# Block sums of phase 2 kept in three PSUM banks, an eleventh weight slot and new planner rules in a fused attention and MLP kernel

## The chip, the cores and the metric

The kernel runs on one core of a Trainium2 chip. The metric is the device time of one execution in microseconds; the median of several runs is compared. The engines are PE (TensorE, matrix products), DVE (VectorE), ACT (ScalarE), POOL (GpSimd) and SP (SyncE, which issues the DMAs).

## The reference

Windowed causal attention with a linear bias per head, then two blocks of dense layers on its 2304 rows. All inputs are float64.

```python
# q, k, v: 4 batches, 8 heads, 576 positions, 64 channels
mask = (rel >= 0) & (rel < 128)
scores = np.where(mask, q @ k.T / 8 - slope[h] * abs(rel), -1e9)
attn = softmax(scores)
x = (attn @ v) as (2304, 512)
h = (x @ w1) * (x @ w2) @ w3          # 512 -> 1024, 1024 -> 1024
x = h @ w_out                         # 1024 -> 512
h = np.maximum(x @ w_in, 0)           # 512 -> 2048
out = h * h @ w_out2                  # 2048 -> 512
```

## The kernel before

**How the work is tiled.** Every tile has 128 partitions. A product of two matrices that must be exact to about float32 is written by `mm3` (L170) as three matmuls on parts called hi and lo (L171 to L173: hi by hi, hi by lo, lo by hi). The weights arrive as float64 words and are turned into float32 on the chip: `conv_g` on ACT (L294), `conv_s` on DVE or ACT (L296), `conv_m` on DVE (L309); a copy (L176, L224) makes hi, and a subtraction (`sub`, L179) makes lo.

**Attention** takes the 32 heads in 16 pairs, `add_pair` (L499). A pair of heads has on PE the scores qk (L428, three pieces, 64 rows of contraction), for each head nine transposes of the exponentials (`p_tr`, L444, in two parts, 4 and 5), and pv (L460, two halves, 64 output columns); on DVE the row maxima (`l_min`, L395), row sums (L410, L411) and scaling (L218), on ACT the exponentials (L403) and the copies of the transposes (`l_pt`, L176). In the same stretch PE forms the product w3 times w_out (`p_w34`, L564): 64 products of 128x128 by 128x512, each in two passes that show as two instructions. It reads the words' converted halves in place, so every other 32-bit word of a row of `raw`. PE's other filling there is batch 0 of x @ w1, x @ w2 and their product with w3·w_out.

**Phase 1** (from about 239 us) does the same for batches 1 to 3 with seven block products instead of eight (Strassen-Winograd): `add_sab` (L968) sums them in three PSUM banks al, be and ga; ACT copies a bank into the buffer d while PE goes on in another, and DVE adds the copies (L1008) and multiplies (L1014). The combined weight blocks are made by `add_wmake` (L897): `combine` (L773) adds 256-column blocks on DVE or POOL, whichever the planner takes.

**Phase 2** (from about 484 us) has two kinds of groups that `add_group` (L1053) writes. The 24 r groups (j, m) compute relu(x @ w_in) for 384 tokens a block, each with seven products P1 to P7 of six matmuls. The nine o groups compute the second layer for 256 columns, 24 matmuls a product. `add_group` gives each product a PSUM bank X of its own (six in all); ACT copies P1's bank (c1), and DVE makes the four blocks of the result by seven additions (L1083): u2 = c1 + P6, u3 = u2 + P7, u4 = u2 + P5, c22 = u4 + P7, c11 = c1 + P2, c12 = u4 + P3, c21 = u3 + P4. For r, ACT then takes the relu of each block in place (L1109), and SP stores it (`s_scr`); the o groups load it again into fo, square it (L1161 and L1147) and split it into words ww or st. In the first o group each product is cut in two (Q and P), so that its first part can run before the last words are ready.

**The order of the work.** All of it is put in order by `Plan` (L32 to L126). A task has a rank, a cost on each engine that may take it (`w_mm`, `w_tt`, `w_act`, ... , L229 to L249), the tasks it depends on, and the buffers it takes and gives back. `run` steps through time: among the tasks that could start within LOOK = 0.1 of the earliest, the one with the lowest rank is next, on the engine where it ends first. The number of buffers for each tag is a table ahead (L253). The engines then run their instructions in exactly this order. `RANK["h0"] + 20.0 * m` is the rank of the m-th pair of heads, `RANK["w34"]` that of the words for L564.

Of the kernel before, what the change touches and what calls it, by code (L numbers as in the profile page):

```python
# [15 lines left out]
RANK = dict(w34=5.49, h0=-13.66, w12=35.93, w12s=7.96, w12l=7.68, mg=500, mgs=4, yl=8, yn=0)  # L16
# [7 lines left out]
NE = 3  # L24
# [3 lines left out]
OM = 3  # L28


class Plan:
# [7 lines left out]
    LOOK = 0.1  # L39

# [15 lines left out]
    def run(self):  # L56
# [14 lines left out]
        order = []  # L71
        while ready:
            cands = []
            for n in ready:
# [29 lines left out]
            _, _, fn, deps, takes, gives, _ = tasks[n]  # L104
            ready.remove(n)
# [18 lines left out]
        assert len(order) == len(tasks), [n for n in tasks if n not in end][:20]  # L124
# [4 lines left out]
def fused_kernel(  # L129
# [119 lines left out]
    def w_dma(kb, n=1):  # L249
# [4 lines left out]
            u=10, u34=4, wo=4, qk=2, v=2, e=NE, p4=4, s=4, t=1, pt=NE, a=1, g=2, asb=2, gf=2, gt=8, ye=2,  # L254
            al=2, be=2, ga=2, d1=2, d2=2, d4=2, gq=8, xs=2, xm=1, xt1=1, xt2=1, yA=14, yB=6, s0=1, t2a=1, t2b=1, v6=6, st=2, c1=2, U2=1, U4=1, U3=1, C=4, X=6, fo=4, fq=5, ww=4,
# [16 lines left out]
    def slot(tag="u"):  # L272
        p, n = (wp, 10) if tag == "u" else (p34, 4)
        return p.tile([128, 2, 1024], F32R, tag=tag, bufs=n, name="wu")

    def w_load(key):
# [4 lines left out]
        else:  # L281
            t = wp.tile([128, 1024, 2], U32, tag="u", bufs=10, name="raw")
# [42 lines left out]
    def add_words(key, rank, tag, users, keep, lead, side=False):  # L325
# [5 lines left out]
        add("cn" + k, rank, {"D": 1.16}, lambda e: conv_m(key, flat(raws[key]) if side else None), ["cg" + k, "cs" + k])  # L331
# [157 lines left out]
    def p_warm():  # L489
        t = ps_t.tile([128, 512], F32, tag="t", name="t")  # L490
        for _ in range(4):
            nc.tensor.matmul(t[:, 0:256], ident, bm[:, 0], start=True, stop=True)
# [6 lines left out]
    def add_pair(m, rank):  # L499
# [17 lines left out]
        for g, w in enumerate((448, 512, 192)):  # L517
            add(f"qk{g}_{m}", r + 1, {"pe": w_nat(w) + 0.1}, lambda e, g=g: p_qk(m, g), [f"ldq{n}" for n in heads] + last,
# [22 lines left out]
        for g, w in enumerate((640, 384)):  # L541
            add(f"pv{g}_{m}", r + 8, {"pe": w_nat(w) + 0.1}, lambda e, g=g: p_pv(m, g),
# [15 lines left out]
    def p_w34(fi, c):  # L558
# [3 lines left out]
        wl = f(raws["w3", fi][:, c * 128:(c + 1) * 128, 0])  # L562
        wr = f(raws["wo", c // 2][:, (c % 2) * 512:(c % 2) * 512 + 512, 0])
# [139 lines left out]
    PO = (1, 6, 7, 5, 2, 3, 4)  # L703
# [7 lines left out]
    def open_q1():  # L711
# [185 lines left out]
    def add_wmake(fi, b, users, rank, prev):  # L897
# [5 lines left out]
        for i in range(4):  # L903
            add(f"cb{i}{z}", rank, w_tt(256), lambda e, i=i: combine("A", i, M, Sg, e),
                ["mb" + z] + [[], [f"cb0{z}"], [f"cb0{z}"], [f"cb1{z}"]][i], [], ["st" + z])
        for part, w in (("a", 1024), ("b", 768)):
# [132 lines left out]
    def p_r(j, m, P):
        o = p_bank(("r", j, m), P, TN)  # L1040
        wh, wl = w_of("i", m, P)
        for c in range(2):
            y = yo[j, P, c]
            mm3(o, wh[:, 128 * c:128 * c + 128], wl[:, 128 * c:128 * c + 128], y[:, 0], y[:, 1], c == 0, c == 1)

    def p_o(t, P, c0=0, c1=NM):
        o = p_bank(("o", t), P, 256) if c0 == 0 else bank[("o", t), P]
        a = ow[t, P]
        for c in range(c0, c1):
            bh, bl = w_of("o", c, P)  # L1050
            mm3(o, a[:, 0, 128 * c:128 * c + 128], a[:, 1, 128 * c:128 * c + 128], bh, bl, c == 0, c == NM - 1)

    def add_group(g, n, order, prod, fin, rank):  # L1053

        z = "".join(str(x) for x in g)
        lastq = list(lastp)
        w = 24 * w_mm(256) if g[0] == "o" else 6 * w_mm(TN)
        for nm, k in (("c1", 2), ("U2", 2), ("U3", 1), ("U4", 2)):
            hold(nm + z, nm, k)
        for c in ("11", "12", "21", "22"):  # L1060
            hold(f"C{c}{z}", "C", 1)
        for i, P in enumerate(order):
            deps, gives, fn = prod(P)
            hold(f"X{P}{z}", "X", 2 if P == 7 else 1)
            if g == ("o", 0):
                add(f"Q{P}{z}", rank + i, {"pe": 18 * w_mm(256)}, lambda e, P=P: p_o(0, P, 0, 6),
                    [d for d in deps if d[-2:] not in ("o6", "o7")] + [lastq[0]], [f"X{P}{z}"])
                lastq[0] = f"Q{P}{z}"
# [290 lines left out]
```

## Time and profile before

| | |
|---|---|
| runs | 857.64, 858.53, 858.99 us; median 858.53 us |
| profiled execution | 858.35 us; span of its trace 856.6 us, mean granted clock 0.992 |
| PE busy | 830.9 us (97%), 5808 matmuls |
| DVE, ACT, POOL busy | 676.9 (79%), 473.6 (55%), 118.4 us (14%) |
| DMA | 139 MB, mean 162 GB/s |

The span runs from the first to the last instruction. An engine's busy time says how long it had work in it; where PE's is short of a stretch, something made it wait. A granted clock of 1.00 is 2.4 GHz, one of 0.50 is 1.2 GHz.

### The profile page before, as it was taken

Reading aid. Unit: us, or ns where it says so; the run is one execution under the profiler, and the core shown is the slowest. Engines: PE = TensorE matmul, PEld = TensorE weight load, DVE = VectorE, ACT = ScalarE, POOL = GpSimd, SP = SyncE. Lnnn points to the kernel's source line nnn. Section 1 sums busy time; section 2 is a strip of 40 time slices with the busy share of each in tenths; the row PEclk is TensorE's granted clock in tenths of the full one; section 3 lists DMA queues with packets and bytes.
Section 4 is the critical chain, followed back from the end, with each engine's and each line's share of the span. In section 5 each row is a group of like instructions: output and inputs, shape, how many; then the busy total and the mean of one; then the engine's idle time right before and its main releaser. Section 6 shows DMA issues by size and latency. Waiting matters only on the chain.

```text
span 856.6 us, 15632 instructions
## 1 busy us (share of the span) xinstructions
PE 830.9 (97%) x5808; PEld 755.5 (88%) x5808; DVE 676.9 (79%) x1417; ACT 473.6 (55%) x961; POOL 118.4 (14%) x133
## 2 busy tenths in 40 slices
PE   6899999999999999999999999999999899999998
PEld 4444477877999989999998999999999799999998
DVE  6889898778599897789468798765689988977772
ACT  5856679988733344343144455543676675665440
POOL 1000000000021320040022053230257200000000
PEclk7999999999999999999999999999999999999999
DMA  9875984686542356511124165343686565545210
GB/s 299 312 240 218 286 269 125 201 242 214 209 169 88 95 173 207 191 51 39 53 79 140 49 217 176 127 164 112 205 275 205 163 162 148 156 135 144 85 49 26
DMA packets 92924, 139.17 MB, mean 162 GB/s; under 512 B 8368, under 2 KB 70320, under 8 KB 90800
## 3 DMA queue, kind: packets, MB, share of 16 engines
q1 hardware_dynamic: 92848, 138.18, 50.3%
q8 instruction: 45, 0.74, 0.4%
q14 instruction: 31, 0.25, 0.1%
HBM read 95.29 MB, written 42.86 MB: 161 GB/s over the span
## 4 chain that ended last, share of the span: by engine, by line
PE 79%; DVE 11%; DMA 4%; ACT 3%; issue 3%; POOL 0%; SPq 0%; ACTq 0%; DVEq 0%; POOLq 0%
PE X L173 14%; PE X L171 14%; PE X L172 14%; PE g L564 6%; PE g L171 5%; PE g L173 4%; PE g L172 4%; PE s L428 3%; PE t L444 3%; PE a L460 3%; DMA u<-in_w2io_dram 2%; PE al L985 2%; PE al L987 2%; PE al L986 2%; DVE d L1008 1%
## 5 line engine op out<-in xcount | busy, mean ns | idle before, releaser
L773 POOL TENSOR_TENSOR st<-st 128x256 f32<-128x256 f32 x65 | 57.3, 894 | 250.7 <-DMA st<-m_scrc 77.6
L1109 ACT ACTIVATE C<-C 128x384 f32<-128x384 f32 x96 | 48.2, 522 | 59.6 <-DVE C L1083 33.7
L171 PE MATMUL g<-gt,wu 128*128 128x288 f32 x256 | 76.3, 298 | 0.0
L172 PE MATMUL g<-gt,wu 128*128 128x288 f32 x256 | 75.6, 296 | 0.0
L173 PE MATMUL g<-gt,wu 128*128 128x288 f32 x256 | 75.4, 295 | 0.0
L403 ACT ACTIVATE e<-e,st 128x256 f32<-128x256 f32 (+1 forms) x128 | 60.6, 476 | 17.5 <-DVE st L395 16.8
L1083 DVE TENSOR_TENSOR C<-X,U 128x384 f32<-128x384 f32 (+1 forms) x99 | 50.6, 518 | 22.4 <-PE X L173 19.4
L172 PE MATMUL X<-yA,u 128*128 128x384 f32 x192 | 65.0, 339 | 0.0
L171 PE MATMUL X<-yA,u 128*128 128x384 f32 x192 | 65.0, 339 | 0.0
L564 PE MATMUL g<-raw 128*128 128x512 f32 x128 | 63.7, 626 | 1.4 <-DVE raw L309 1.4
L173 PE MATMUL X<-yA,u 128*128 128x384 f32 x192 | 65.0, 339 | 0.0
L985 PE MATMUL al<-x,wc 128*128 128x288 f32 x192 | 57.8, 301 | 3.6 <-ACT d L176 3.6
L176 ACT ACTIVATE ww<-fq 128x1024 fp32r<-128x1024 f32 x35 | 37.0, 1059 | 38.2 <-PE X L173 28.2
L986 PE MATMUL al<-x,wc 128*128 128x288 f32 x192 | 56.6, 295 | 0.3 <-DVE x L179 0.3
L987 PE MATMUL al<-x,wc 128*128 128x288 f32 x192 | 56.8, 296 | 0.0
L172 PE MATMUL X<-u,ww 128*128 128x256 f32 x198 | 55.4, 280 | 0.0
L173 PE MATMUL X<-u,ww 128*128 128x256 f32 x198 | 55.4, 280 | 0.0
L171 PE MATMUL X<-u,ww 128*128 128x256 f32 x198 | 55.4, 280 | 0.0
L395 DVE CUSTOM_DVE_ANT_0 e<-s,bm 128x256 f32<-128x256 f32 (+1 forms) x128 | 43.7, 387 | 13.3 <-PE s L428 8.0
L176 ACT ACTIVATE d<-al 128x288 f32<-128x288 f32 x72 | 29.1, 409 | 41.6 <-PE al L987 32.8
L179 DVE TENSOR_TENSOR ww<-fq,ww 128x1024 fp32r<-128x1024 f32 x35 | 42.8, 1222 | 11.0 <-ACT ww L176 10.7
L171 PEld LDWEIGHTS g<-gt,wu 128*128 128x128 f32 x256 | 48.1, 188 | 0.8 <-issue 0.8
(216 smaller groups left out, 2728.3 us busy)
## 6 DMA issues: line engine op xcount, KB each, us to landing
s_scr<-C SPq DMA_DIRECT2D x96, 192.0 KB, 2.2
u<-in_w2io_dram SPq DMA_DIRECT2D x26, 512.0 KB, 6.1
fo<-s_scr SPq DMA_DIRECT2D x20, 512.0 KB, 4.3
qk<-in_qk_dram SPq DMA_DIRECT2D x32, 288.0 KB, 5.2
st<-m_scrc SPq DMA_DIRECT2D x18, 512.0 KB, 3.7
raw<-in_w3t_dram SPq DMA_DIRECT2D x8, 1024.0 KB, 7.7
raw<-in_w_dram SPq DMA_DIRECT2D x8, 1024.0 KB, 9.0
fq<-s_scr SPq DMA_DIRECT2D x16, 512.0 KB, 4.3
```

The lines of the kernel that those rows point to most:

```text
L171: nc.tensor.matmul(o, wh, xh, start=start, stop=False)
L172: nc.tensor.matmul(o, wh, xl, start=False, stop=False)
L173: nc.tensor.matmul(o, wl, xh, start=False, stop=stop)
L176: nc.scalar.activation(out=o, in_=i, func=ACTF.Copy)
L403: nc.scalar.activation(out=e, in_=e, func=ACTF.Exp, bias=st[:, 0, i:i + 1], scale=-1.0, accum_out=st[:, 1, i:i + 1],)
L564: nc.tensor.matmul(gw[fi], wl, wr, start=c == 0, stop=c == 7)
L773: ENG[e].tensor_tensor(out=o, in0=a, in1=b, op=op)
L985: nc.tensor.matmul(o, wh, xh, start=start and c == 0, stop=False, skip_group_check=True)
L986: nc.tensor.matmul(o, wh, xl, start=False, stop=False, skip_group_check=True)
L987: nc.tensor.matmul(o, wl, xh, start=False, stop=c == 1, skip_group_check=True)
L1083: nc.vector.tensor_tensor(out=t_(o, tag), in0=bank[g, P], in1=cs[g, i], op=ALU.add)
L1109: nc.scalar.activation(out=x, in_=x, func=ACTF.Relu)
```

## The change

In phase 2, `add_group` keeps three banks instead of seven: P1 goes to bank xa, and P6, P5 and P3 are added to it by PE itself; P7 goes to xb, P4 is added; P2 goes to xc. Before PE adds the next product to xa, ACT or DVE copies what stands there (c1, u2 and u4), and the last copy is c12, for r with the relu in it. DVE then has three additions a group (c22, c11, c21). In the last r group and the first o group P4 has a bank xd in place of the second half of xb, and four additions. The products' order is now 1, 2, 6, 7, 5, 3, 4. One more weight slot is paid for by one p4 buffer and one xs buffer less; the first o group's second word takes it. `conv_m` writes the words of w3 and w_out side by side. The planner charges 0.11 for a change between the tile shapes of qk, pv and the rest and then stays with a shape, and before its time 40 it fills gaps on PE of over 1 us with small products (`filler`, 11 in all). Pairs of heads are 12 ranks apart instead of 20 and begin at -20, the words for L564 at 4. Two more o words (m = 3, 4) are not merged ahead of time. `combine` in `add_wmake` is tied to DVE: of 72 such additions 32 were on POOL.

```diff
-RANK = dict(w34=5.49, h0=-13.66, w12=35.93, w12s=7.96, w12l=7.68, mg=500, mgs=4, yl=8, yn=0)
+RANK = dict(w34=4, h0=-20, w12=35.93, w12s=7.96, w12l=7.68, mg=500, mgs=4, yl=8, yn=0, hs=12)
-OM = 3
+OM = 5
...
+    SWITCH = 0.11
+    STAY = 60
+    FILL = 40.0
...
+        shape = lambda n: {"qk": 1, "pv": 2}.get(n[:2], 0)
...
+                    if e == "pe" and shape(n) != now:
+                        w += self.SWITCH
+                    elif e == "pe" and now:
+                        rank -= self.STAY
...
+            if e == "pe":
+                now = shape(n)
+                idle = t - free.get(e, t)
+                if 1.0 < idle and t < self.FILL:
...
+                            tasks[k] = (0, {}, lambda e, tag=tag, idle=idle: self.filler(tag, int((idle - 0.4) / 0.24), 128), (), (), (), 0)
...
-            u=10, u34=4, wo=4, qk=2, v=2, e=NE, p4=4, s=4, ...
+            u=11, u34=4, wo=4, qk=2, v=2, e=NE, p4=3, s=4, ...
-            ... v6=6, st=2, c1=2, U2=1, U4=1, U3=1, C=4, X=6, ...
+            ... v6=6, st=2, xa=2, xb=2, xc=2, D1=2, D2=2, D4=2, D3=1, ...
...
-        add("cn" + k, rank, {"D": 1.16}, lambda e: conv_m(key, flat(raws[key]) if side else None), ["cg" + k, "cs" + k])
+        add("cn" + k, rank, {"D": 1.16}, lambda e: conv_m(key, flat(raws[key])), ["cg" + k, "cs" + k])
...
-        wl = f(raws["w3", fi][:, c * 128:(c + 1) * 128, 0])
-        wr = f(raws["wo", c // 2][:, (c % 2) * 512:(c % 2) * 512 + 512, 0])
+        wl = f(flat(raws["w3", fi]))[:, c * 128:(c + 1) * 128]
+        wr = f(flat(raws["wo", c // 2]))[:, (c % 2) * 512:(c % 2) * 512 + 512]
...
-            add(f"cb{i}{z}", rank, w_tt(256), ...
+            add(f"cb{i}{z}", rank, w_tt(256, "D"), ...
...
+        for nm, tag in (("xa", "xa"), ("xb", "xb"), ("xc", "xc"), ("C11", "D1"), ("C21", "D2"), ("C22", "D4"), ("C12", "D3")):
+            hold(nm + z, tag, 1)
+        steps = [
+            (1, "xa", [], True), (2, "xc", [], True), (6, "xa", ["c1"], False), (7, "xb", [], True),
+            (5, "xa", ["u2"], False), (3, "xa", ["u4"], False), (4, "xb", ["c22"], False),
+        ]
+        if last:
+            hold("xd" + z, "xc", 1)
+            p4 = (4, "xd", [], True)
+            steps = [*steps[:2], steps[3], p4, steps[2], *steps[4:6]] if g[0] == "r" else [*steps[:2], p4, *steps[2:6]]
+        for i, (P, nm, dep, first) in enumerate(steps):
             deps, gives, fn = prod(P)
...
+            deps = deps + [d + z for d in dep] + {6: [f"P1{z}"], 5: [f"P6{z}"], 3: [f"P5{z}"], 4: [f"P7{z}"]}.get(P, [])
...
+        def cp(e, c, tag, func=None):
+            t = cs[g, c] = new(tag, [128, TN])[:, 0:n]
+            if func:
+                nc.scalar.activation(out=t, in_=bank[g, "xa"], func=func)
+            else:
+                copy(e, t, bank[g, "xa"])
+
+        for nm, P, c, tag in (("c1", 1, "11", "D1"), ("u2", 6, "21", "D2"), ("u4", 5, "22", "D4")):
+            add(nm + z, -30, w_copy(n, True), lambda e, c=c, tag=tag: cp(e, c, tag), [f"P{P}{z}"], [f"C{c}{z}"])
...
+        plus("c22", "22", "xb", ["u4", "P7"], [], -30)
+        plus("c11", "11", "xc", ["c1", "P2"], ["xc"], -20)
+        if last:
+            plus("d21", "21", "xb", ["u2", "P7", "c22"], ["xb"], -20)
+            plus("c21", "21", "xd", ["d21", "P4"], ["xd"], -20)
+        else:
+            plus("c21", "21", "xb", ["u2", "P4", "c22"], ["xb"], -20)
+        if g[0] == "r":
+            add("c12" + z, -20, w_act(n), lambda e: cp(e, "12", "D3", ACTF.Relu), [f"P3{z}"], [f"C12{z}"], [f"xa{z}"])
...
-            tag = "st" if P in (1, 2) else "ww"
+            tag = "u" if (t, P) == (0, 2) else "st" if P in (1, 2) else "ww"
...
-        add_pair(m, RANK["h0"] + 20.0 * m)
+        add_pair(m, RANK["h0"] + RANK["hs"] * m)
```

The planner's order shows in the instructions. PE at the program's start, before, behind the warming product L492: L428 is a piece of qk, L444 transposes, L564 the first product of w3 and w_out.

```order
L428 MATMUL s<-qk 128x128 x2
L428 MATMUL s<-qk 128x256 x6
L428 MATMUL s<-qk 128x192 x2
L444 MATMUL t<-ident,e 128x128 x4
L444 MATMUL t<-ident,p_140 128x128 x2
L444 MATMUL t<-ident,e 128x128 x7
L428 MATMUL s<-qk 128x128 x2
L428 MATMUL s<-qk 128x256 x2
L444 MATMUL t<-ident,p_141 128x128 x2
L444 MATMUL t<-ident,e 128x128 x3
L428 MATMUL s<-qk 128x256 x4
L564 MATMUL g<-raw 128x512
```

The first product of w3 and w_out stands after one pair's scores, two heads' transposes and most of the next pair's scores.

PE at the start, with the change (L515, L451, L467, L483 and L589 are the same lines, moved):

```order
L515 MATMUL t<-bm,ident 128x256 x4
L451 MATMUL s<-qk 128x128 x2
L451 MATMUL s<-qk 128x256 x6
L515 MATMUL t<-bm,ident 128x128 x2
L451 MATMUL s<-qk 128x192 x2
L451 MATMUL s<-qk 128x128 x2
L451 MATMUL s<-qk 128x256 x6
L467 MATMUL t<-ident,e 128x128 x4
L451 MATMUL s<-qk 128x192 x2
L467 MATMUL t<-ident,p_138 128x128 x2
L467 MATMUL t<-ident,e 128x128 x3
L515 MATMUL g<-bm,ident 128x128 x3
```

The second pair's scores have moved ahead of the second head's transposes, small fillers (L515) have come in, and the first product of w3 and w_out (L589) stands only 18 rows below these, after the third pair's scores and the first pv.

DVE in the r groups, before, one group from its first addition (U and c are the intermediate sums, X the banks):

```order
L1083 TENSOR_TENSOR U_6601<-X,c_6591 128x384
L1083 TENSOR_TENSOR U_6610<-X,U_6601 128x384
L1083 TENSOR_TENSOR U_6619<-X,U_6601 128x384
L1083 TENSOR_TENSOR C<-X,U_6619 128x384
L1083 TENSOR_TENSOR C<-X,c_6591 128x384
L1083 TENSOR_TENSOR C<-X,U_6619 128x384
L1083 TENSOR_TENSOR C<-X,U_6610 128x384
```

Three of the seven make intermediate sums, and four of them read one.

DVE in the r groups, with the change, two groups (D holds the copies and becomes the result):

```order
L1122 TENSOR_TENSOR D_6303<-xb,D_6303 128x384
L1122 TENSOR_TENSOR D_6287<-xb,D_6287 128x384
L1122 TENSOR_TENSOR D_6312<-xc,D_6312 128x384
L1122 TENSOR_TENSOR D_6366<-xb,D_6366 128x384
L1122 TENSOR_TENSOR D_6350<-xb,D_6350 128x384
L1122 TENSOR_TENSOR D_6375<-xc,D_6375 128x384
```

A group has three additions where it had seven, and none of them adds onto another.

ACT in the r groups, before: c1's copy, and relus (L1109) between conversions of the stage.

```order
L176 ACTIVATE c_7179<-X 128x384
L1109 ACTIVATE C<-C 128x384
L1147 ACTIVATE fo<-fo 128x1024
L176 ACTIVATE u<-s_7013 128x1024
L176 ACTIVATE v_7234<-s_7013 128x768
L1109 ACTIVATE C<-C 128x384 x2
L176 ACTIVATE u<-st 128x1024
```

Only the copy of P1 (c) reads a bank here.

ACT in the r groups, with the change (L199 the copies of xa, L1113 the copy with the relu in it, L1152 the other relus):

```order
L199 ACTIVATE D_6350<-xa 128x384
L199 ACTIVATE D_6366<-xa 128x384
L199 ACTIVATE D_6375<-xa 128x384
L1152 ACTIVATE D_6366<-D_6366 128x384
L1113 ACTIVATE D_6384<-xa 128x384
L1152 ACTIVATE D_6350<-D_6350 128x384
L1152 ACTIVATE D_6375<-D_6375 128x384
```

Seven instructions of a group follow one another on ACT, four of which read xa between PE's products into it.

## Rows read from the trace of the kernel before

**Rows 1.** Groups of the page: busy us of each engine (share of the span) x instructions.
```profile
PE 830.9 (97%) x5808; PEld 755.5 (88%) x5808; DVE 676.9 (79%) x1417; ACT 473.6 (55%) x961; POOL 118.4 (14%) x133
```

**Rows 2.** Stretches: us; busy of PE, PEld, DVE, ACT, POOL; PEclk; DMA; GB/s.
```profile
6.40:28.00 21.60, 16.60 (x87) 10.51 (x86) 16.24 (x61) 15.50 (x45) 0.00 (x0) 0.76 0.91 305
28.00:53.00 25.00, 21.81 (x116) 11.85 (x117) 23.02 (x61) 19.49 (x45) 0.80 (x2) 1.00 0.75 284
...
115.00:239.00 124.00, 123.48 (x1015) 101.44 (x1014) 98.03 (x401) 106.64 (x319) 1.33 (x3) 1.00 0.67 205
239.00:484.00 245.00, 237.82 (x1759) 234.01 (x1758) 200.61 (x371) 93.14 (x184) 43.10 (x44) 1.00 0.34 114
484.00:667.00 183.00, 183.00 (x1052) 183.00 (x1052) 137.51 (x229) 99.18 (x182) 66.42 (x63) 1.00 0.53 177
667.00:680.00 13.00, 9.13 (x56) 8.60 (x56) 12.74 (x15) 8.27 (x12) 2.83 (x3) 0.87 0.36 108
```

**Rows 3.** PE waits: engine, tile, line, releaser: us in total, times, longest.
```profile
PE al L985 <- ACT d L176: 3.6, 5, 1.2
```

**Rows 4.** Timeline of DVE, 8 to 17 us: start, us, engine, line, operation, tiles.
```profile
8.21 0.29 DVE L395 CUSTOM_DVE_ANT_0 e<-s,bm 128x128 f32<-128x128 f32 x1 [3.13 <-PE s L428]
...
14.06 0.17 DVE L410 TENSOR_SCALAR st<-st 128x5 f32<-128x5 f32 x1
...
15.93 0.69 DVE L303 TENSOR_SCALAR raw<-raw 128x1024 uint32<-128x1024 uint32 x1
16.54 1.22 DVE L309 SCALAR_TENSOR_TENSOR raw<-raw 128x1024 uint32<-128x1024 uint32 x1
```

**Rows 5.** Groups by line and shape: count, busy us, mean ns, idle before.
```profile
L773 DVE TENSOR_TENSOR st<-st 128x256 f32<-128x256 f32 x51 | 21.8, 460 | 2.0 <-DMA st<-m_scrc 1.7
...
L176 ACT ACTIVATE c<-X 128x384 f32<-128x384 f32 x24 | 11.6, 482 | 3.0 <-PE X L173 2.9
```

**Rows 6.** Groups by line and shape, PE, 6.4 to 53 us.
```profile
L564 PE MATMUL g<-raw 128*128 128x512 f32 x28 | 15.0, 641 | 1.4 <-DVE raw L309 1.4
```

**Rows 7.** Timeline of PE, transposes and a pv half.
```profile
41.47 0.76 PE L460 MATMUL a<-pt,v 128*64 128x192 f32 x8
...
44.20 0.60 PE L444 MATMUL t<-ident,e 128*128 128x128 f32 x4
44.63 1.07 PE L564 MATMUL g<-raw 128*128 128x512 f32 x2
```

**Rows 8.** Timeline of PE, qk visits between products of w3 and w_out.
```profile
56.05 11.97 PE L564 MATMUL g<-raw 128*128 128x512 f32 x26
67.95 1.79 PE L428 MATMUL s<-qk 64*128 64x128 f32 x16
69.67 2.08 PE L564 MATMUL g<-raw 128*128 128x512 f32 x4
71.68 0.60 PE L428 MATMUL s<-qk 64*128 64x192 f32 x4
72.20 1.18 PE L564 MATMUL g<-raw 128*128 128x512 f32 x2
```

**Rows 9.** Timeline of DVE and POOL, 311 to 317 us.
```profile
311.89 0.45 DVE L224 CAST x<-xm 128x576 fp32r<-128x576 f32 x1
...
316.47 1.00 DVE L224 CAST x<-xm 128x576 fp32r<-128x576 f32 x1
...
314.99 2.17 POOL L773 TENSOR_TENSOR st<-st 128x256 f32<-128x256 f32 x2
```

**Rows 10.** Timeline of phase 1, 455 to 460 us, PE and ACT.
```profile
456.08 0.39 ACT L176 ACTIVATE d<-al 128x288 f32<-128x288 f32 x1
...
456.53 0.40 PE L985 MATMUL al<-x,wc 128*128 128x288 f32 x1 [1.04 <-ACT d L176]
...
457.30 0.30 PE L987 MATMUL al<-x,wc 128*128 128x288 f32 x1
...
457.69 0.41 ACT L176 ACTIVATE d<-al 128x288 f32<-128x288 f32 x1 [1.22 <-PE al L987]
```

More of the change, by code (lines that the diff above doesn't have):

```diff
@@ L71, in run @@
         order = []
+        shape = lambda n: {"qk": 1, "pv": 2}.get(n[:2], 0)
+        now = 0
         while ready:
@@ L123, in run @@
                     ready.add(u)
-        assert len(order) == len(tasks), [n for n in tasks if n not in end][:20]
+        assert len(order) == len(tasks) and len(end) + sum(n[:4] == "fill" for n in tasks) == len(tasks), [n for n in tasks if n not in end][:20]
         return order
@@ L323, in flat, with add_words @@
         return r.rearrange("p n w -> p (n w)")[:, 0:1024]
-    def add_words(key, rank, tag, users, keep, lead, side=False):
+    def add_words(key, rank, tag, users, keep, lead):
         k = "%s%d" % key
@@ L487, in t_xs, with p_warm @@
         nc.sync.dma_start(out=x_scr[b][p], in_=xt[b, p])
[L489 to L492, printed above, removed]
+    def p_warm(tag="t", k=4, w=256):
+        t = (ps_t if tag == "t" else ps_g).tile([128, 512], F32, tag=tag, name=tag)
+        for _ in range(k):
+            nc.tensor.matmul(t[:, 0:w], ident, bm[:, 0, 0:w], start=True, stop=True)
+    plan.filler = p_warm
     hold("warm", "t", 1)
@@ L517, in add_pair @@
         for g, w in enumerate((448, 512, 192)):
-            add(f"qk{g}_{m}", r + 1, {"pe": w_nat(w) + 0.1}, lambda e, g=g: p_qk(m, g), [f"ldq{n}" for n in heads] + last,
+            add(f"qk{g}_{m}", r + 1, {"pe": w_nat(w)}, lambda e, g=g: p_qk(m, g), [f"ldq{n}" for n in heads] + last,
                 [f"s{g}_{n}" for n in heads], [f"qk{m}"])
@@ L1050, in p_o, with add_group @@
             bh, bl = w_of("o", c, P)
[L1051 to L1053 removed]
+            mm3s(o, a[:, 0, 128 * c:128 * c + 128], a[:, 1, 128 * c:128 * c + 128], bh, bl, start and c == 0, c == NM - 1)
+    def add_group(g, n, prod, fin, rank, last=False):
         z = "".join(str(x) for x in g)
[L1056 removed]
         w = 24 * w_mm(256) if g[0] == "o" else 6 * w_mm(TN)
[L1058 to L1062, printed above, removed]
[L1063 to L1093 removed]
@@ new lines, in add_group, with go @@
+        for i, (P, nm, dep, first) in enumerate(steps):
+            deps, gives, fn = prod(P)
+            deps = deps + [d + z for d in dep] + {6: [f"P1{z}"], 5: [f"P6{z}"], 3: [f"P5{z}"], 4: [f"P7{z}"]}.get(P, [])
+            if P == 1 and lastp[0]:
+                deps = deps + lastp
+            if P == 1:
+                lastp[0] = f"P1{z}"
+            def go(e, P=P, nm=nm, first=first, fn=fn, **kw):
+                if first and not kw.get("c0"):
+                    bank[g, nm] = new("xc" if nm == "xd" else nm, [128, 512])[:, 0:n]
+                fn(bank[g, nm], first, **kw)
+            if g == ("o", 0) and P in (1, 2):
+                add(f"Q{P}{z}", rank + i, {"pe": 0.75 * w}, lambda e, go=go: go(e, c0=0, c1=6),
+                    [d for d in deps if d[-2:] not in ("o6", "o7")], [nm + z])
+                add(f"P{P}{z}", rank + i, {"pe": 0.25 * w}, lambda e, go=go: go(e, c0=6, c1=NM), deps + [f"Q{P}{z}"], [], gives)
+            else:
+                add(f"P{P}{z}", rank + i, {"pe": w}, go, deps, [nm + z] if first else [], gives)
@@ new lines, in cp, with plus @@
+        def cp(e, c, tag, func=None):
[6 more added lines that the diff above has]
+            add(nm + z, -30, w_copy(n, True), lambda e, c=c, tag=tag: cp(e, c, tag), [f"P{P}{z}"], [f"C{c}{z}"])
+        def plus(nm, c, b, deps, gives, rank):
+            def fn(e):
+                nc.vector.tensor_tensor(out=cs[g, c], in0=bank[g, b], in1=cs[g, c], op=ALU.add)
+            add(nm + z, rank, w_tt(n, "d"), fn, [d + z for d in deps], [], [b + z for b in gives])
@@ L1189, in add_o @@
             early = -30 if t == 0 and P in (1, 2) else 0
-            add(f"oh{P}{t}", rank + pos + early, w_act(1024), hi, [src[P]] + ([] if tag == "st" else ["q2"]) + (["wlao6", "wlbo6"] if t == 0 and tag == "st" else [])
+            add(f"oh{P}{t}", rank + pos + early, w_act(1024), hi, [src[P]] + ([] if tag != "ww" else ["q2"]) + (["wlao6", "wlbo6"] if t == 0 and tag != "ww" else [])
                 + chain[P], [f"ow{P}{t}"], F(k))
```

93 lines of the change are left out of this document (43 added, 50 removed).

## The prediction

> **What bounds the kernel now.** The first thing to read is the page's line of engines: PE (TensorE) is busy 830.9 us of a span of 856.6 [rows 1]. So the time can fall only where PE idles, runs at its lower clock, or spends longer on an instruction than its columns need. Next comes the table of stretches, to find where that is [rows 2]. Three stretches hold nearly all of it. From 6.4 to 28 us PE is busy 16.60 of 21.60 us at a mean granted clock of 0.76 (1.2 GHz for part of it), and to 53 us another 21.81 of 25.00. From 239 to 484 (phase 1) it idles 245 - 237.82 = 7.2 us. From 667 to 680, where phase 2 turns from the r groups to the o groups, it is busy 9.13 of 13.00 at 0.87. The r groups (484 to 667) keep PE busy all of 183.00 us. Read last, the list of PE's waits says who ends phase 1's idle times: first of all ACT's copies of its sums, 3.6 us in five waits [rows 3].
>
> The sum is made against the profiled execution, 858.35 us (span 856.6 plus 1.75 around it), 0.18 under the median of 858.53. About 0.2%, or 1.7 us, is what a measurement here can tell from no change.
>
> **The change, part by part.** PE loses no product and gains 11 small filler matmuls, so every term is idle time or overhead.
>
> *Start.* In the old order PE takes the first w3·w_out product (L564) after two pairs of heads have begun; in the new one three pairs of qk, almost four heads' transposes and one pv pair come first. What PE must wait for is DVE. Its prices: ten row maxima of two heads from 8.21 to 11.74, 1.76 per head; row sums and scaling of a head from 14.06 to 15.93, 1.87; a word conversion 0.69 and 1.22 [rows 4]. Ahead of the conversion of the fourth w_out word (cnwo3), the new DVE order has 41 maxima (14.5), scaling for 7.5 heads (14.0), six and seven of the two conversion steps (12.7) and six adds to x, taken at 0.46 like the adds of [rows 5] (2.8): 44.0 us from 8.21, so about 52 us. By then PE has all that needs neither this word nor later ones. Counted against what PE did by 53 in the old trace (28 L564 instructions, so 14 products of two each [rows 6]; likewise three qk pairs and six heads' transposes), that is nine transposes for each of two heads more, about 1.0 per head (four take 0.43), one second pv half at about 0.8 [rows 7], the first pieces of two qk pairs at 1.72 and one last piece at 0.5, and three products fewer at 2 x 0.458 [rows 8]: 2.0 + 0.8 + 3.44 + 0.5 - 2.75 = 4.0 us of work. PE is full from 53 on, so work done earlier comes off the end: **-4.0**. Bounds: 0, if ACT's exponentials (busy 35 of these 46.6 us) replace DVE as the gate, and -8.6, all 8.2 us idle of 6.4 to 53 and a little of the lower clock. The four groups of fillers stand in idle gaps ahead of the first product and count as nothing; without a gap each would cost two or three short matmuls.
>
> *Fewer changes of tile shape.* The planner now charges a change between qk's (64 rows), pv's (64 columns) and the full tile, and PE makes 114 instead of 126. A row prices one: 26 L564 take 11.90 us, 0.458 each; four between two qk visits take 71.68 - 69.67 = 2.01 where 1.83 would do, so 0.18 [rows 8]. 12 x 0.18 = **-2.2**; bounds -1 and -3.
>
> *Later attention.* With pairs 12 instead of 20 ranks apart and filled from earlier, the same exponentials, copies and maxima fall into some 205 us instead of 233; ACT then has about 84% and DVE 90%, as ACT has now from 115 to 239 (106.64 of 124, with PE idle only 0.5) [rows 2]. **+1.5**, between 0 and +6.
>
> *w3 and w_out words side by side.* L564 costs 0.458 us for 512 columns; if it went at the rate of the r groups' products (183.00 us for 1052, nearly all of 384 columns [rows 2]: 0.453 ns per column, four times that for the four passes of one product, 1.81 ns, against 1.79 now) it gains nothing; at that of the qk visits it gains 2.9 us: the visit of 16 takes 1.72 us and the one of four 0.52 [rows 8], so 1.20 us for the 704 columns between them (two heads run side by side), 1.70 ns, and 0.09 x 512 x 64 products is 2.9 us. I take **-1.0**; bounds 0 and -2.9. The Trainium skill (SBUF — State Buffer, in "Door 1: The DMA port swizzle") says that reads run at full bandwidth with two hits per 16-byte line, and so that up to four fp32 words may be strided for free; every other word would then cost nothing, and the forecast would be 1.0 higher. The rows above cannot tell 0 from 2.9.
>
> *Phase 1.* All 72 of its 256-column combinations are now on DVE, 32 more than before: 32 x 0.46 [rows 5] = 15 us on an engine with 200.61 of 245 busy [rows 2]. Against that POOL makes none of them any more: while POOL adds (from 314.99) DVE's cast takes 1.00, without it 0.45 [rows 9]. POOL's 43.1 us in this stretch slow DVE by up to as much, so the exchange should at least pay for itself, and 3.6 us of PE waiting for ACT's copies here are late DVE work handed on [rows 3]. **-2.0**; bounds -6 and +5.
>
> *r groups.* Seven banks with seven adds become three chains: P1, P6, P5, P3 in one, P7, P4 in another, P2 alone. DVE has 95 adds fewer of 168; ACT has 72 copies more and 24 relus fewer, which are folded into the last copy. DVE's relief is worth nothing here, since PE has no idle time [rows 2]. But P5 now waits for ACT's copy after P6, and P3 for the one after P5: 48 waits that did not exist. One product of another bank lies between, six matmuls of 0.174 = 1.05 us. The hand-over costs 0.09 (PE's end at 457.60 to ACT's start at 457.69) plus 0.48 (copy of 384 columns) plus 0.06 (copy's end at 456.47 to PE's start at 456.53) [rows 5, 10]: 0.63, so 0.4 us are free unless ACT is at something else. Its longer pieces, copies of 1024 columns, can be in front. Phase 1 already hands over in this way, and loses 7.2 us over 24 groups. I take **+1.5** (two or three collisions in every ten groups), bounds 0 and +9.8, a whole rate of 0.2 for each hand-over. The eleventh u slot frees its loads sooner; PE waits for none there: 0.
>
> *The turn.* o's first two products now run in part ahead of r's last, and P4 has a bank of its own; but P6 and P5 of o's first group stand behind DVE, which splits the same words. Idle of 3.9 us and 0.13 x 13 = 1.7 us for the lower clock [rows 2] become idle of about 4.8, an estimate from three conversions and splits in a row on DVE, and one on ACT: **-0.8**, between -4 and +3.
>
> *o groups, end.* One o product is 24 matmuls of 256 columns, at 0.453 ns a column 2.8 us, against a hand-over of 0.6: 0. The last add stays.
>
> Sum: -4.0 - 2.2 + 1.5 - 1.0 - 2.0 + 1.5 - 0.8 = -7.0, so 858.35 - 7.0 = 851.35, **851.4 us**; bounds of the terms, not all at one end, give 844 to 857.
>
> **The rivals.** *The chain decides (slower).* The 48 hand-overs of the r groups wait for ACT: each copy is queued behind a conversion of 1024 columns or a relu, as ACT works 99.18 of 183 us here already and gets 72 copies more for 24 relus fewer, about 48 x 0.48 = 23 us. At 0.3 us each they cost 14.4 instead of 1.5: 851.4 + 12.9 = 864.3. At 0.18 each, 8.5 over all, the whole gain is gone. For it: phase 1's waits. Against it: the planner gives these copies the first rank, and 0.4 us of each is covered. *The start gives nothing.* Heads taken first only bring ACT and DVE to their limit later, the 4.0 comes back as waits between 100 and 210, and the fillers are not enough to raise the clock: 851.4 + 4.0 and 1.5 more of the later waits = 856.9, about the same as before. For it: ACT is 86% busy from 115 to 239. Against: PE has no idle time there now, and the words are converted as early as before to within a few us. *More goes than I count.* The losses of phase 1 (7.2 us) and of the turn (5.6) go to half, and the L564 take their whole 2.9: 851.4 - (3.6 - 2.0) - (2.8 - 0.8) - 1.9 - 5.0, the last from the start's lower clock and idle time, = 840.9. That needs DVE to be freed from POOL's adds by more than the 15 us that it takes over.
>
> **How the numbers follow.** The forecast 0.50 (844 to 857, all but its last 0.2 us faster); the chain 0.17; no gain at the start 0.17, two thirds of it within 1.7 us of before; more than counted 0.16. From 841 to 862 leaves out half of the chain's case and half of the largest gain, some 0.17. Faster by over 0.2%: 0.50 + 0.16 + 0.03 = 0.69; same 0.12; slower 0.17 + 0.02 = 0.19.
>
> **What would show it.** Right: PE's busy time within 3 us of 830.9; more qk and transposes and fewer L564 before 53 us; idle in phase 1 under 5 us; r groups at 183 to 185 us; L564 at about 0.45 each. Wrong: PE waiting for ACT's copy of xa in most r groups (the chain), or PE waits on pt or e between 100 and 210 us that together pass 3 us (the start), or a stretch 239 to 484 that is longer than before. A time over 858 or under 844 makes the forecast wrong.

## The result, and the profile after

The changed kernel takes 846.04 us (median; 845.36 to 847.64) against 858.09 in the same comparison: a ratio of 0.9862 (95% interval 0.9843 to 0.9881), 12 us. The direction and the range were as forecast; the gain is 12 where 7.0 were expected. The profiled execution took 845.38 us, with a span of 843.4.

The page's line of engines, to be read beside [rows 1]:

```profile
PE 823.2 (98%) x5830; PEld 752.8 (89%) x5830; DVE 629.7 (75%) x1354; ACT 494.3 (59%) x1026; POOL 61.1 (7%) x75
```

DVE lost 47 us of work and POOL 57, ACT gained 21. PE has 22 matmul records more (the fillers) and is busy 7.7 us less, for two reasons that the experiments show: a better clock and the words side by side. The table of stretches, with the bounds moved to the changed kernel's stages (columns as in [rows 2]):

```profile
6.40:28.00 21.60, 19.02 (x145) 14.05 (x145) 19.81 (x85) 19.39 (x61) 0.00 (x0) 1.00 0.95 291
28.00:53.00 25.00, 23.98 (x147) 13.98 (x145) 23.43 (x75) 23.34 (x59) 0.60 (x1) 1.00 0.85 276
...
115.00:239.00 124.00, 122.03 (x943) 99.89 (x942) 100.82 (x337) 88.68 (x254) 3.05 (x7) 1.00 0.71 218
239.00:477.00 238.00, 234.79 (x1754) 232.99 (x1753) 186.24 (x374) 84.33 (x171) 27.44 (x21) 1.00 0.28 94
477.00:660.00 183.00, 181.26 (x1030) 179.91 (x1029) 112.70 (x183) 123.45 (x235) 22.82 (x24) 1.00 0.55 183
660.00:672.00 12.00, 9.23 (x76) 8.82 (x75) 10.59 (x11) 8.73 (x12) 0.00 (x0) 1.00 0.83 227
```

The first row says most: before 28 us ACT and DVE are busy nine tenths of the time instead of three quarters, PE has 145 matmuls (22 of them fillers) where it had 87, and the granted clock is 1.00 where it was 0.76. The last row's clock is 1.00 as well (it was 0.87), in this execution: its mean granted clock is 0.999, that of the other three 0.998.

Three marks of PE's timeline divide the span: the last product of batch 0 with w1 and w2 (g<-x), the last y product of phase 1 (g<-gt), and the last product of all.

| | before | after | difference | terms of the sum |
|---|---|---|---|---|
| end of batch 0's products | 257.7 | 248.6 | -9.1 | -4.0 -2.2 +1.5 -1.0 = -5.7 |
| phase 1 from there | 233.5 | 228.4 | -5.1 | -2.0 |
| phase 2 from there | 362.2 | 363.4 | +1.2 | +1.5 -0.8 = +0.7 |
| after the last product | 3.3 | 3.1 | -0.2 | 0 |
| span | 856.6 | 843.4 | -13.2 | -7.0 |

PE's longer waits (columns as in [rows 3]; all of the span), and PE's stretch from the start of phase 2 to the turn:

```profile
PE t L467 <- ACT pt L199: 2.5, 6, 0.6
PE xa L1063 <- DVE ww L202: 2.1, 1, 2.1
PE xa L1061 <- ACT D L199: 1.8, 2, 1.4
PE al L1010 <- ACT d L199: 1.4, 1, 1.4
PE s L451 <- DVE st L418: 1.3, 3, 0.6
```

```profile
477.00:653.80 176.80, 176.43 (x996) 175.14 (x994) 106.77 (x177) 119.45 (x229) 22.82 (x24) 1.00 0.57 187
```

The 48 new hand-overs of the r groups hardly show: PE waits noticeably for a copy of xa (D) twice in the whole span, and one of those, 1.4 us up to 655.2 us, is in the turn. From 477 to 653.8 us PE is idle for 0.4 us in all.

### The profile page after: what moved, and what is told of

The parts are those of the page before. It is cut to its first block, busy times and chain, and to the rows that moved or that the text cites. A ratio compares the mean times of both kernels' runs of the same rounds, so it can differ in the third digit from the quotient of the medians.

```text
span 843.4 us, 15493 instructions
## 1 busy us (share of the span) xinstructions
PE 823.2 (98%) x5830; PEld 752.8 (89%) x5830; DVE 629.7 (75%) x1354; ACT 494.3 (59%) x1026; POOL 61.1 (7%) x75
## 4 chain that ended last, share of the span: by engine, by line
PE 76%; DVE 16%; ACT 4%; issue 2%; DMA 1%; POOL 0%; SPq 0%; ACTq 0%; DVEq 0%; POOLq 0%
PE xa L1061 8%; PE xa L1063 8%; PE xa L1062 8%; PE g L194 6%; PE g L195 6%; PE g L196 6%; PE xb L1061 4%; PE xb L1063 4%; PE xb L1062 4%; DVE e L418 3%; PE al L1010 3%; PE al L1012 2%; PE al L1011 2%; PE xc L1062 2%; PE xc L1061 2%
## 5 line engine op out<-in xcount | busy, mean ns | idle before, releaser
L1122 DVE TENSOR_TENSOR D<-xb,D 128x384 f32<-128x384 f32 (+1 forms) x66 | 34.0, 518 | 58.5 <-PE xb L1063 29.7
L199 ACT ACTIVATE D<-xa 128x384 f32<-128x384 f32 (+1 forms) x102 | 46.3, 455 | 39.2 <-PE xa L1063 36.5
L589 PE MATMUL g<-raw 128*128 128x512 f32 x128 | 62.6, 604 | 0.3 <-DVE raw L332 0.3
L202 DVE TENSOR_TENSOR ww<-fq,ww 128x1024 fp32r<-128x1024 f32 x34 | 41.6, 1223 | 23.1 <-ACT ww L199 22.7
L199 ACT ACTIVATE ww<-fq 128x1024 fp32r<-128x1024 f32 x35 | 37.0, 1058 | 34.7 <-PE xa L1063 19.7
L1152 ACT ACTIVATE D<-D 128x384 f32<-128x384 f32 x72 | 37.1, 523 | 25.5 <-DVE D L1122 25.4
L199 ACT ACTIVATE ye<-g 128x288 f32<-128x288 f32 x32 | 13.1, 410 | 66.0 <-PE g L196 61.9
L798 DVE TENSOR_TENSOR st<-st 128x256 f32<-128x256 f32 (+1 forms) x105 | 41.7, 428 | 11.1 <-DMA st<-m_scrc 6.1
L199 ACT ACTIVATE d<-al 128x288 f32<-128x288 f32 x72 | 29.2, 410 | 33.9 <-PE al L1012 26.1
L195 PEld LDWEIGHTS g<-gt,wu 128*128 128x128 f32 x256 | 48.3, 189 | 0.0
L196 PEld LDWEIGHTS g<-gt,wu 128*128 128x128 f32 x256 | 48.2, 188 | 0.0
L194 PEld LDWEIGHTS g<-gt,wu 128*128 128x128 f32 x256 | 48.1, 188 | 0.1
L451 PE MATMUL s<-qk 64*128 64x256 f32 (+2 forms) x320 | 42.6, 369 | 2.5 <-DVE st L418 1.3
L483 PEld LDWEIGHTS a<-pt,v 128*64 128x64 f32 x384 | 23.6, 136 | 19.2 <-issue 5.9
```

What stands on the lines that cost most here:

```text
L194: nc.tensor.matmul(o, wh, xh, start=start, stop=False)
L195: nc.tensor.matmul(o, wh, xl, start=False, stop=False)
L196: nc.tensor.matmul(o, wl, xh, start=False, stop=stop)
L199: nc.scalar.activation(out=o, in_=i, func=ACTF.Copy)
L589: nc.tensor.matmul(gw[fi], wl, wr, start=c == 0, stop=c == 7)
```

## The experiments

In each comparison the kernel before was run on the same chip, with a median of 856.9 to 857.1 us; so ratios are compared. The changed kernel stands at 0.9862, which at 857 is 845.2. Marks are those of each kernel's one profiled execution.

| kernel | ratio to before (95%) | batch 0 ends | phase 1 | phase 2 |
|---|---|---|---|---|
| changed | 0.9862 (0.9843 to 0.9881) | 248.6 | 228.4 | 363.4 |
| words_apart | 0.9880 (0.9864 to 0.9896) | 248.7 | 228.4 | 365.3 |
| no_fillers | 0.9885 (0.9870 to 0.9900) | 249.1 | 228.3 | 364.2 |
| no_shape_rule | 0.9898 (0.9879 to 0.9916) | 251.2 | 228.2 | 364.8 |
| old_ranks | 0.9925 (0.9911 to 0.9940) | 253.7 | 228.0 | 366.1 |
| old_start | 0.9956 (0.9940 to 0.9972) | 252.2 | 228.8 | 365.1 |
| combos_any | 0.9918 (0.9903 to 0.9933) | 248.5 | 232.6 | 364.9 |
| old_merges | 0.9919 (0.9906 to 0.9932) | 248.2 | 230.7 | 366.7 |
| six_merges | 0.9901 (0.9886 to 0.9915) | 247.4 | 229.6 | 367.4 |
| ten_slots | 1.0031 (1.0017 to 1.0044) | 256.4 | 232.8 | 365.5 |
| seven_banks | 1.0081 (1.0061 to 1.0102) | 255.2 | 232.9 | 370.7 |
| slot_alone (on before) | 1.0096 (1.0077 to 1.0114) | 254.1 | 231.0 | 373.9 |
| banks_alone (on before) | 1.0034 (1.0022 to 1.0046) | 256.7 | 232.8 | 363.3 |

How far the marks of two executions differ by themselves can be read from three pairs in which PE's instructions have the same order: changed and words_apart to the end, and, each to the end of phase 1, before and banks_alone, ten_slots and seven_banks. In the last two pairs batch 0 ends 0.9 and 1.2 us apart. In words_apart, whose edit does not touch phase 2, that phase takes 1.9 us longer: in the turn its clock is at half from 667.4 to 670.8 us, where the changed kernel's stays up, and both wait 2.1 us for the same word there. The clock fell in the turn in nine of these twelve experiments. So a difference of less than about 2 us in a mark is not shown to come from an edit.

**The start: words, fillers, shapes, ranks.**

```diff
-        wl = f(flat(raws["w3", fi]))[:, c * 128:(c + 1) * 128]
-        wr = f(flat(raws["wo", c // 2]))[:, (c % 2) * 512:(c % 2) * 512 + 512]
+        wl = f(raws["w3", fi][:, c * 128:(c + 1) * 128, 0])
+        wr = f(raws["wo", c // 2][:, (c % 2) * 512:(c % 2) * 512 + 512, 0])
```

`conv_m` then writes w3 and w_out in place.

> The changed kernel (846.0 us) with the words of w3 and w_out left every other 32-bit word, as before; every engine's instruction order is the same. If the layout sets the rate of the 128 w3·w_out matmuls, their spacing goes from 0.430 back to 0.451 us and the time to 848.7; if stride is free, spacing and time stay (846.0). The prediction's middle value would be 847.0.

Four matmuls of w3·w_out (two products) without a change of tile between, in PE's timeline, first of the changed kernel, then of words_apart:

```profile
96.62 1.88 PE L589 MATMUL g<-raw 128*128 128x512 f32 x4
98.34 0.60 PE L467 MATMUL t<-ident,e 128*128 128x128 f32 x4
```

```profile
98.31 1.98 PE L589 MATMUL g<-raw 128*128 128x512 f32 x4
100.12 0.60 PE L467 MATMUL t<-ident,e 128*128 128x128 f32 x4
```

From start to start, 1.72 / 4 = 0.430 us side by side and 1.81 / 4 = 0.452 apart: the stride costs 5% of each matmul, 2.9 us over 128. By the Trainium skill (SBUF — State Buffer, "Door 1: The DMA port swizzle") a stride of two fp32 words would be free; the measurement differs. But batch 0 ends only 0.2 us later. PE up to that mark, in the changed kernel and in words_apart (columns as in [rows 2]):

```profile
6.40:248.60 242.20, 235.99 (x1625) 170.68 (x1625) 209.67 (x678) 184.23 (x501) 4.90 (x11) 1.00 0.77 244
6.40:248.70 242.30, 238.36 (x1624) 171.47 (x1624) 209.68 (x678) 184.18 (x501) 4.89 (x11) 1.00 0.76 244
```

PE, being faster with the words side by side, is idle for 6.2 us instead of 3.9. The ratio's interval overlaps the changed kernel's: no gain by itself is shown.

```diff
-  tasks[k] = (0, {}, lambda e, tag=tag, idle=idle: self.filler(tag, int((idle - 0.4) / 0.24), 128), (), (), (), 0)
+  tasks[k] = (0, {}, lambda e: None, (), (), (), 0)
```

> The changed kernel with the filler products not issued, the order of all else the same. If the fillers are what holds the clock at the start, the granted clock falls to 0.50 for a stretch between 8 and 25 us, as before the change, and the time rises by 2.5 to 4 us (848.5 to 850). If the heads' denser work holds it, the clock stays at 1.00 and the time within 1 us of 846.0.

The first two stretches of no_fillers:

```profile
6.40:28.00 21.60, 17.36 (x116) 12.06 (x115) 18.10 (x79) 18.20 (x57) 0.00 (x0) 0.92 0.94 285
28.00:53.00 25.00, 23.73 (x151) 13.98 (x146) 23.33 (x76) 22.84 (x58) 0.59 (x1) 1.00 0.81 255
```

The clock falls to half from 17.7 to 21.1 us, after PE's gaps, where it had fallen from 11.8 to 22.0 before the change. Neither expectation came out whole, and how much of the clock the heads and how much the fillers hold is not told apart. With neither of them (old_start, below) the clock is at half from 13.6 to 20.4 us; with the fillers and the old order of heads (old_ranks, below) it does not fall in the start at all. But banks_alone, which has the start of the kernel before, has it at half from 13.1 to 20.0 only, so 3.4 us more or less can be the execution. Batch 0 ends 0.5 us later without fillers: no gain by them is shown, neither in the trace nor in the time, where the intervals overlap.

```diff
-    SWITCH = 0.11
-    STAY = 60
+    SWITCH = 0.0
+    STAY = 0
```

> The changed kernel without the planner's charge for changes of tile shape and without its staying with a shape; ranks, fillers and the rest as changed. If a change costs 0.18 us, as one row of the kernel before says, each dozen of them costs 2.2 us, and by the prediction's term the time is 848.2; if such changes are hidden or the order matters more, the time is 846.0 within 1 or even less.

PE makes 125 changes of shape instead of 114; the ratio is 0.0036 higher, 3.1 us, with intervals that just overlap, and batch 0 ends 2.6 us later. 11 x 0.18 = 2.0 would be the term's size, so the two agree. The order of everything else changes with it, so the price of one change of shape is not shown by itself. (The change also lowers the planner's cost of a qk piece by 0.1 and of a pv half by 0.05; no run puts these back.)

```diff
-RANK = dict(w34=4, h0=-20, ..., hs=12)
+RANK = dict(w34=5.49, h0=-13.66, ..., hs=20)
```

> The changed kernel with the old ranks of heads and words (pairs 20 apart) and the shape rule and fillers kept. If the early heads make what old_start lost (about 4 us by the end of phase 1, 6.8 in the time), the time is about 852; if the shape rule made it, it is 846 to 848.

In old_start the shape rule and the fillers go too:

> The changed kernel with the old ranks of heads and words (pairs 20 apart), no charge for changes of tile shape, no fillers; phases 1 and 2 as changed. If the start and the attention stage hold most of the gain, as the marks of the two traces say (9.1 us by the end of attention), the time is about 855. If the gain is made by phases 1 and 2, it stays under 850.

The start of old_ranks (columns as in [rows 2]):

```profile
6.40:28.00 21.60, 19.21 (x136) 14.12 (x136) 18.79 (x70) 17.17 (x52) 0.00 (x0) 1.00 0.90 304
28.00:53.00 25.00, 22.59 (x114) 11.89 (x113) 24.20 (x60) 19.26 (x41) 0.00 (x0) 1.00 0.81 308
```

By the mark of batch 0 old_ranks loses 5.1 us and old_start 3.6, in the time 5.4 and 8.1 us. So the early heads are a large part of the start's gain, but not all 9.1 us: with the old start, batch 0 still ends 5.5 us earlier than in the kernel before. And it is not through the clock of the start that the early heads gain: old_ranks has the full clock in these rows and loses the 5.1 us all the same.

**The eleventh slot and the three banks.** seven_banks puts the whole old phase 2 back (its `add_group` as printed above), with ten slots:

```diff
-            u=11, ...  xa=2, xb=2, xc=2, D1=2, D2=2, D4=2, D3=1, ...
+            u=10, ...  c1=2, U2=1, U4=1, U3=1, C=4, X=6, ...
```

> The changed kernel with the old phase 2 (a bank for each product, seven additions, the old order of products) and ten weight slots, which its buffers need. The prediction's terms (r +1.5, turn -0.8) say 845.3; from the end of phase 1 to the end the changed kernel took 1.2 us longer than the one before, which says 844.8. If the three banks save time instead, by what DVE is spared, it is 848 or more.

It is slower than the kernel before, and 6.7 us behind the changed kernel by the end of batch 0 already, where no group of phase 2 has run. What is left to differ there is the slot. So ten_slots:

```diff
-            u=11, ...
+            u=10, ...
-            tag = "u" if (t, P) == (0, 2) else "st" if P in (1, 2) else "ww"
+            tag = "st" if P in (1, 2) else "ww"
```

> The changed kernel with ten weight slots instead of eleven, the first o group's second word back in its old buffer; three banks and all else as changed. If the eleventh slot is what the gain of attention's end and of phase 1 hangs on (with seven_banks, which has ten, batch 0 ended 6.7 us later and phase 1 took 4.5 us longer), the time is 854 to 857. If seven_banks lost that by something else, it is 845 to 847.

Without the slot the rest of the change makes the kernel slower than it was, 14.5 us above the changed kernel, more than the 8 to 11 us expected. Up to the end of phase 1 PE's order is the same as in seven_banks, so the loss up to there does not come from the banks. SP's timeline shows how: the last loads of w1 and w2's words (raw) and the first of w_in and w_out's (u), in the changed kernel:

```profile
113.71 0.59 SPq L312 DMA_DIRECT2D raw<-in_w_dram  x1
127.32 1.24 SPq L773 DMA_DIRECT2D u<-in_w2io_dram  x2
```

and in ten_slots:

```profile
125.89 0.37 SPq L312 DMA_DIRECT2D raw<-in_w_dram  x1
142.84 0.81 SPq L773 DMA_DIRECT2D u<-in_w2io_dram  x2
```

They are issued 12.2 and 15.5 us later: with one slot fewer the planner has them further down SP's order. The first product of batch 0 with w1 and w2 follows at 152.2 us instead of 143.0. PE has heads for that time, since they come early; but then these run out (316 of 320 qk instructions are done by 186 us in both kernels), with too few products of batch 0 between them (84 matmuls by then instead of 96). PE's timeline of ten_slots where it waits, and the stretches around, first of ten_slots, then of the changed kernel:

```profile
188.59 0.69 PE L483 MATMUL a<-pt,v 128*64 128x128 f32 x2 [2.27 <-DVE pt L247]
```

```profile
180.00:190.00 10.00, 7.73 (x58) 6.03 (x57) 6.48 (x25) 5.70 (x17) 0.37 (x1) 0.92 0.70 218
190.00:200.00 10.00, 9.77 (x63) 8.54 (x62) 7.34 (x30) 7.92 (x26) 0.37 (x1) 0.73 0.82 265
```

```profile
180.00:190.00 10.00, 9.98 (x93) 7.89 (x94) 9.11 (x40) 9.89 (x32) 0.00 (x0) 1.00 0.88 294
190.00:200.00 10.00, 10.00 (x87) 9.11 (x86) 9.62 (x31) 9.52 (x25) 0.00 (x0) 1.00 0.54 186
```

After the gap the clock falls too (0.73): 121 matmuls in 20 us against 180. slot_alone asks the reverse, the slot on the kernel before:

```diff
-            u=10, ... p4=4, ... xs=2, ... c1=2, ... C=4, X=6, ...
+            u=11, ... p4=3, ... xs=1, ... c1=1, ... C=3, X=6, ...
```

> The kernel before (858.1 us) with eleven weight slots and nothing else of the change; one p4, one xs, one c1 and one C buffer less pay for it. If the slot makes the gain by itself, batch 0 ends about 251 instead of 257.7 us into the span and phase 1 takes 4 us less, so some 9 us less by the end of phase 1; the r groups, short of two buffers, may give some of that back. If the slot is worth something only with the early heads, the end of phase 1 stays within 2 us of before (491 us).

By the end of phase 1 it is 6.0 us ahead of before (485.1 against 491.1), less than the 9 expected. So at that mark: neither 491.1, the slot alone 485.1, everything but the slot 489.2, both 476.9. 6.0 and 1.9 us apart become 14.2 together: the rest of the change, early heads included, pays only when the words for PE's other work also come early. Its time is worse all the same. In the turn PE waits 7.6 us for ACT, and the clock is at half for 10.2 us:

```profile
PE X L171 <- ACT st L176: 7.6, 1, 7.6
```

The likely reason, which no run isolates, is the buffers that it gave up for phase 2.

Three banks against seven, with ten slots on both sides, is ten_slots against seven_banks: 1.0031 against 1.0081, 4.3 us for the banks, all behind the end of phase 1. Not the hand-overs but the turn decides. The stretch 652 to 690 us, first with seven banks, then with three:

```profile
652.00:690.00 38.00, 28.43 (x168) 26.95 (x168) 37.52 (x48) 25.14 (x36) 13.98 (x12) 0.87 0.54 167
```

```profile
652.00:690.00 38.00, 34.05 (x222) 33.00 (x221) 34.53 (x44) 30.60 (x43) 5.51 (x5) 0.96 0.59 176
```

With seven banks DVE is busy 37.52 of 38 us there and PE waits 7.2 us for one word; with three DVE has some spare time.

```profile
PE X L194 <- ACT st L199: 7.2, 1, 7.2
```

The two runs put the whole of the new phase 2 at 4.3 us, its order of products and the separate bank for P4 included; DVE's relief by itself is not isolated. And with the banks alone (phase 2's hunks of the diff on the kernel before):

> The kernel before (858.1 us) with the three banks of phase 2 and nothing else of the change; the order is the same up to phase 2. The prediction's terms (r +1.5, turn -0.8) give 858.8, with PE waiting for ACT's copies of xa in two or three of ten r groups. What ten_slots and seven_banks differ by says the banks save 4 us in the turn when o words 3 and 4 are merged late; here they are merged early, so that saving should be small: 856 to 858. If the hand-overs decide, it is 864 or more.

The ratio is 1.0034, 2.9 us slower, outside the 856 to 858 expected. PE waits 1.9 us for copies of xa in four places, only one of them (0.2 us) in the r groups, far from two or three in ten; its profiled execution, 2.0 us faster than its median, is 1.6 us ahead of before at the end of phase 1, with the same instructions, and takes 1.1 us more in phase 2. The mean granted clock is 0.996 in that execution and 0.992 to 0.994 in the other six, so they lose at least part of the rest at half clock; where, their times don't say. So on the kernel before, where o words 3 and 4 were merged early, the banks bring nothing.

**Phase 1.** combos_any gives the planner POOL back, old_merges puts o words 3 and 4 back:

```diff
-            add(f"cb{i}{z}", rank, w_tt(256, "D"), ...
+            add(f"cb{i}{z}", rank, w_tt(256), ...
```

> The changed kernel with phase 1's 256-column combinations on DVE or POOL as the planner likes. By the prediction's term this gives back 2.0 us (848.0), with phase 1 at 230.4 and DVE's instructions slower beside POOL's. If it doesn't matter, 846.0 within 0.8 and phase 1 at 228.4.

```diff
-OM = 5
+OM = 3
```

> The changed kernel with o words 3 and 4 merged ahead of time again, in phase 1, instead of in the r groups. If phase 1 was relieved by moving them, it takes 1 to 2 us longer (228.4 before this edit) and the turn gets no worse, total 846 to 848. If their place does not matter, 846.0 within 0.8.

Phase 1 takes 4.2 and 2.3 us longer; the second is little more than two executions differ by themselves, but the time of old_merges is 4.9 us longer, clear of the changed kernel's interval and of the 846 to 848 expected. PE's waits in phase 1, combos_any, then the changed kernel:

```profile
PE be L1010 <- DVE d L1033: 3.6, 2, 2.5
PE al L1010 <- ACT d L199: 1.4, 2, 0.9
```

```profile
PE al L1010 <- ACT d L199: 1.4, 1, 1.4
PE be L1010 <- DVE d L1033: 1.2, 2, 1.1
```

With POOL busy 36.8 us instead of 27.4, PE waits 2.4 us more for DVE's sums, and behind one such gap the clock was at half from 305.3 to 308.7 us. DVE's busy time of phase 1 is 178.4 us in combos_any and 177.9 in the changed kernel although it has fewer adds: other instructions were slower, as [rows 9] shows for a cast of the kernel before. The 16 subtractions of 1024 columns that split combined weights take 1298 ns each in combos_any and 1223 in the changed kernel. With ten slots DVE is busy 186 us there, and PE's waits for ACT's copies are 4.2 us in eight places, where the changed kernel has 1.4 in one. In old_merges the turn does get worse, which was not expected: phase 2 takes 3.3 us longer, with the clock at half from 667.2 to 674.0 us and these waits for o's words, where the changed kernel has 0.6 and 2.1 us:

```profile
PE xa L1061 <- ACT ww L199: 3.7, 1, 3.7
PE xa L1063 <- DVE ww L202: 1.5, 1, 1.5
```

Last, a step further in the same direction:

> The changed kernel with a third o word (m = 5) no longer merged ahead of time. old_merges showed 4.4 us for two words; if moving work from phase 1 to the r groups pays as long as DVE has room there (112 of 183 us busy), this gains another 1 to 2 us (844 to 845). If the r groups or the turn now wait for the word, it is 847 or more.

It loses 3.3 us: phase 1 is no shorter, and PE waits for copies of xa in six places, 4.0 us. ACT is no busier in the r groups than before this edit (122.9 us against 123.5 of 183), so the order is the likely cause there; which piece of it was not tried. The clock is also at half for 3.4 us in phase 1 and for 3.4 us in the turn. Of the three values the changed kernel's is the best, and no version faster than the changed kernel was found.

## Why the prediction was right, and where its sizes were wrong

**Start, -4.0.** The mechanism was right, the size was not. By 53 us PE has done 36 qk instructions (of 20 a pair), 18 transposes and 12 of pv (of 24 a pair) more, and one product less: at 1.72 + 0.52 a pair for qk and about 2.0 for pv that is 4.0 + 2.0 + 1.0 - 0.9 = 6.1 us. What the step left out is the clock: 10.2 us at half speed, with 7.65 us of busy PE in them, are gone. Heads or fillers, the runs do not tell apart which removed them (no_fillers still has 3.4 us of it, old_ranks none). The bound of -8.6 had that in it. The fillers, taken at nothing, are not shown to be worth more.

**Shapes, later attention, words: -1.7 together.** What is left of the 9.1 is -3.0. The shape rule agrees with its term (2.6 us at the mark, 2.2 expected). From 115 to 180 us ACT was busy 57.0 of 65 us and PE 63.1, so the later attention costs about what was said. Of the words' 2.9 us nearly nothing came off the end, where -1.0 was expected. For the whole 9.1 us there is one sum: PE runs the same instructions up to that mark in both kernels, fillers aside. Before the change:

```profile
6.40:257.70 251.30, 241.82 (x1603) 171.76 (x1603) 207.68 (x672) 183.51 (x497) 6.53 (x9) 0.98 0.72 233
```

Idle time fell from 9.5 to 6.2 us and busy time by 5.8, and busy time is where the clock, the words and the changes of shape act. How these three share it is not told apart.

**"The eleventh u slot frees its loads sooner; PE waits for none there: 0."** This is the step that failed. It looked for PE waiting on a load of the kernel before and found none, but in the changed kernel the heads come first, and the slot decides whether batch 0's weights are ready when the heads run out. Its absence costs 14.5 us, more than the whole gain. What was booked as the start's gain hangs on it. That the time still fell into the range, 2 us above its lower end, is therefore partly luck: a part on which the whole gain depends stood at nothing.

**Phase 1, -2.0.** Measured -5.1. combos_any bears out the mechanism (DVE's instructions slow beside POOL's) at twice its size, 4.2; that o words moved out of phase 1 was not in the sum at all (2.3), and the slot counts here too (4.4). These three add to 10.9, twice what was measured, so they overlap.

**r groups, +1.5; turn, -0.8.** Phase 2 took 1.2 us more, the sum said 0.7. The hand-overs leave 0.4 us of idle time before the turn, not 1.5: the 0.4 us that were free in each were nearly always enough. (The upper bound there is 48 times 0.2, which is 9.6 and not 9.8.) The turn is idle 4.4 us, about as estimated (4.8), at full clock in this execution. By that it gained 1.2 us, so the rest of phase 2 took 2.4 us more, and where stays open. "DVE's relief is worth nothing here" was true of the r groups and wrong of what it permits: the new phase 2 has room for the two o words and is worth 4.3 us in the turn, with ten slots on both sides.

**The rivals.** The chain did not decide. That the start gives nothing fell with old_start. The largest gain, 841, went too far: phase 1 gave what it said, the turn did not. Among the signs, PE's busy time fell by 7.7 us, not under 3: a better clock shows as less busy time. In combos_any matmuls of 288 columns start 0.24 us apart at half clock (306 to 308 us) and 0.13 us apart at full clock. The words count too: in words_apart PE is busy 827.0 us against 823.2.

## What to carry to other kernels

An extra buffer is not priced by who waits for it now, but by what the new order will want to have ready: run the change without it. A part that is worth nothing or a loss by itself (the three banks; all but the slot) may pay with the others, so both "the change without it" and "it alone" belong to a study. And where a planner writes the order, each undoing also draws another order: the undoings here cost far more together than the change gained, so the price of one is not the worth of its part.

## What was not expected of the hardware

- PE's fp32 matmuls of 512 columns start every 0.430 us from words side by side and every 0.452 us from every other word (changed kernel and words_apart), with the same instructions in the same order.
- The granted clock fell to half not only at the start but after single gaps in the middle (2.3 us before 188.5 us in ten_slots, 2.5 us before 305.3 us in combos_any), and stayed there for 6.8 and 3.4 us, while PE had work again. A gap of 2.4 us in no_shape_rule (210.8 us) and one of 2.1 us in the changed kernel's turn (664.5 us) brought no fall, so the gap alone does not decide.
